# The turn between two passes: joins ahead of the values' low parts, b22's high parts earlier on ScalarE

## The chip, the core and the metric

The kernel runs on one core of a Trainium2 chip. The core has TensorE (PE, matrix products, written into eight PSUM banks of 128x512 fp32), VectorE (DVE), ScalarE (ACT), GpSimd (POOL) and SyncE (SP); each has its own queue of instructions and works through it in order. Data is moved by DMAs, issued from the queues of SP, ScalarE and GpSimd. The metric is the device time of one execution, in microseconds (us).

## The reference

```python
x = A_x                                              # 2048 tokens, 512 wide
g = sigmoid((x * gate_w).sum(-1, keepdims=True))
qkv = x @ wqkv                                       # 32 heads of 16 each
# each token attends to 8 keys: itself and those 2, 4, .. 14 tokens back
a = softmax(q . k * 16 ** -0.5) @ v, then @ wo
b = (gelu(x @ w_gate) * (x @ w_up)) @ w_down         # 1792 hidden
return g * a + (1 - g) * b
```

All inputs and outputs are fp32.

## The kernel before

**Accuracy.** TensorE is fed fp32r operands. Each fp32 operand is split into a high part (ScalarE copies it, rounded, into an fp32r tile: `hi`) and a low part (VectorE subtracts the high part from the original: `lo`), and each product takes three matmuls: high x high, low x high, high x low.

**Two passes.** The even tokens (`par` 0) go first, the odd ones (`par` 1) second. Each pass has a projection of keys and queries, then a feed-forward part, `ffn(par)`, over 14 chunks of 128 hidden columns. The projection of the values and the gate (`values`, matmuls on line 130) is spread over the first two chunks of `ffn`, the down projection over the later ones. Attention for a pass is VectorE work (scores on lines 212 and 215, the mix with the values on lines 260 to 268, a transpose on 273). It is written as one generator in small pieces, and `pull(budget)` issues the next pieces at many places among the matmuls. Most pieces are tied to a matmul (`paced`), so that they don't run before it, and have a lower priority than the code around them.

**Seven products in place of eight.** Both the keys/queries projection and the gate/up products treat their operand as a 2x2 matrix of blocks and make four block results from seven products, of sums of blocks (a scheme of Strassen's kind). The blocks of the tokens are a11, a12, a21, a22, and s1 to s4 are sums of them; those of the weights are b11, b12, b21, b22, and t1 to t4 are sums of them. The products are a11·b11, a12·b21, s1·t1, s2·t2, s3·t3, s4·b22 and a22·t4.

**The turn.** `kq_second()` makes the keys and queries of the second pass, between `ffn(0)` and `ffn(1)`. `ready()`, interleaved with the last down projections of `ffn(0)`, makes its first operands. `block(ps, a, w, ...)` issues one product: four PSUM banks, one for each 128 tokens, with six matmuls each, 24 in all. The seven blocks run in this order:

1. a11·b11 into U (banks `acc0` to `acc3`); ScalarE copies U to V_ (four `p` banks)
2. a12·b21, added to V_; V_ holds keys and queries of the first half of heads, `put` evicts it with ScalarE
3. s2·t2, added to U; ScalarE copies the sums to u2 (four `hl` tiles)
4. s3·t3, added to U; ScalarE copies the sums to u3 (four `hh` tiles)
5. a22·t4, added to U, evicted by `put` too
6. s1·t1 into Z_ (four `p` banks); VectorE adds u3 to it (`join(1, BT + t, Z_[t], u3[t])`): these are the first joins, "the sixth product's sums"
7. s4·b22, added to Z_; VectorE adds u2 (`join(1, t, Z_[t], u2[t])`): the second joins

Each `join` writes its result over the `hh` or `hl` tile, and two DMAs on GpSimd's queue store it. Block 7 adds to the same banks that the first joins read, so its first matmul on a bank comes behind the join of that bank. After block 7 TensorE goes on with the values of the second pass (line 130) and the first chunk of `ffn(1)` (line 432), whose PSUM banks are those that the second joins free.

**What sets the order.** The framework orders the instructions of each engine when the kernel is built, by their place in the program, their priority and a simulated timeline. On top of it three chains are written out by hand: `row` for VectorE, `act` for ScalarE and `mms` for TensorE (class `Row`) keep the instructions issued through them in program order on their engine. All of the turn's splits, subtractions, evictions, joins and blocks go through these chains, so all have line 760 in the profile. Attention pieces aren't in the chains, and the framework places them between.

**The values' weights.** `values_raw` loads the raw weights of a chunk kc into a `c` tile, `values_room` takes a `d` tile for its high and low parts. There are four `d` tiles; the first two chunks get theirs after t2's product, the last two after t1's.

**Buffers that matter here.** `g1` has two buffers. In the turn b11 has one and t4 the other; b22 takes b11's after block 1. s3 and s4 take the room of raw weights that are used up: s4's second pair takes that of b22.

Of the kernel before, what the change touches and what calls it, by code (L numbers as in the profile page):

```python
# [21 lines left out]
KC = D // P  # L22
# [26 lines left out]
def tile_gated_mix(ctx: ExitStack, tc: tile.TileContext, xt, wqkv, wff, wo, out):  # L49
# [11 lines left out]
    def tl(tag, dt=F32):  # L61
        return pool.tile([P, COLS.get(tag, 512)], dt, name=tag, bufs=BUFS[tag])
# [5 lines left out]
    def bank(tag):  # L68
        return psum.tile([P, 512], F32, name=tag, bufs=BUFS.get(tag, 1))
# [67 lines left out]
    def take_first(par, ps, jj, copy):  # L137

        if par not in KQ:
            KQ[par] = pool.tile([P, 3 * NP - 1, UC], F32, name="kq")  # L140
        st = tl(next(stages))[:, :CU].rearrange("p (a d) -> p a d", a=2)
        two = ps.rearrange("p (a c d) -> p c a d", a=2, c=2)
        copy(KQ[par][:, NP - 1 + jj::NP], two[:, 0])
        copy(st, two[:, 1])
        for a, t in enumerate((KS[par, 0][1, W:], QS[par, 0][1])):
            nc.sync.dma_start(t.rearrange("(p j) d -> j p d", j=NP)[jj], st[:, a])

    def shift(par, queue, i, j):
        k = KQ[par][:, :2 * NP - 1]
        if not i:  # L150
            nc.gpsimd.memset(k[:1, :NP - 1], 0.0)
        for a, b in (1, P - 15), (P - 15, P):
            queue.dma_start(k[a:b, i:j], k[a - 1:b - 1, NP + i:NP + j])

    def rows(t, jj):
        return t.rearrange("c (p j) d -> j p c d", j=NP)[jj]
# [206 lines left out]
    def fetch_d(f):  # L363
        RD[f] = tl("r")
        nc.sync.dma_start(RD[f], wff[f, :, 1024:])
# [43 lines left out]
    def fetch_sums(f):  # L409
        RAW[f] = tl("raw")  # L410
        nc.sync.dma_start(RAW[f][:, 5 * QW:7 * QW], WS[f, 1])
        q = wff[f, :, :1024].rearrange("p (a c) -> p a c", c=QW)
        nc.sync.dma_start(RAW[f].rearrange("p (a c) -> p a c", c=QW)[:, 4::3], q[:, 1::2])
# [354 lines left out]
    SRC, OP_, Q2, RAWS = {}, {}, {}, {}  # L768

    def slots(tag, n, w=512):  # L770
        t = tl(tag, F32R)
        return [t[:, i * w:i * w + 512] for i in range(n)]

    def pairs(rooms_):
        return [tuple(rooms_[2 * k:2 * k + 2]) for k in range(2)]

    def name(n, ops, srcs=None):
        for k in range(2):
            OP_[n, k], SRC[n, k] = ops[k], srcs[k] if srcs else ops[k][1].bitcast(F32)

    def halves(t):
        return t[:, :512], t[:, 512:1024]

    def hi(n, k):
        return act.activation(OP_[n, k][0], SRC[n, k], AF.Copy)

    def lo(n, k):
        h, l = OP_[n, k]
        row.tensor_tensor(l, SRC[n, k], h.bitcast(F32), op=OP.subtract)

    def both(f, *ns):
        for n in ns:
            for k in range(2):
                f(n, k)

    def sub(o, a, b):
        row.tensor_tensor(o, a, b, op=OP.subtract)
# [4 lines left out]
    def block(ps, a, w, first, kcs=(0, 1), ask=0.0):  # L802
        for t in range(BT):
            for kc in kcs:
                ah, al = OP_[a, kc]
                wh, wl = OP_[w, kc]
                for n, (a_, w_) in enumerate(((ah, wh), (al, wh), (ah, wl))):
                    mm(ps[t], t, a_, w_, first and kc == 0 and n == 0, kc == 1 and n == 2)
            if ask:
                pull(ask)  # L810

    def out_of(o, ps):
        act.activation(o, ps, AF.Copy)

    def join(par, jj, ps, s):
        row.tensor_tensor(s, ps, s, op=OP.add)
        two = s.rearrange("p (a c d) -> p a c d", a=2, c=2)
        queue = nc.gpsimd if par else nc.sync
        queue.dma_start(rows(KS[par, 1][:, W:], jj), two[:, 0])
        queue.dma_start(rows(QS[par, 1], jj), two[:, 1])  # L820
# [16 lines left out]
    def load(n, i, t, m):  # L837
        nc.sync.dma_start(tiled(t, m), TS[n][i:i + m].rearrange("i p c -> p i c"))
# [218 lines left out]
    def load_pairs(n):  # L1057
        t = [tl("d", F32R) for _ in range(2)]
        for k in range(2):
            OP_[n, k] = t[k][:, :512], t[k][:, 512:1024]  # L1060
            load(n, 2 * k, t[k], 2)
# [35 lines left out]
    def kq_second():  # L1097
        for _ in Q2["turn"]:
            pass
        q, s12 = Q2["q"], Q2["s12"]  # L1100
        t4 = slots("g1", 4)
        name("t4", pairs(t4), halves(RAWS["b21"]))
        U = [bank(f"acc{t}") for t in range(BT)]
        for k in range(2):
            X[1, 1, k] = tl("rt", F32R), tl("rt", F32R)
        name("a21", [X[1, 1, k] for k in range(2)], [q[k][2] for k in range(2)])

        block(U, "a11", "b11", True, ask=ASK[0])
        V_ = [bank("p") for _ in range(BT)]
        for t in range(BT):  # L1110
            out_of(V_[t], U[t])
        both(hi, "a22")
        both(hi, "t3")
        both(lo, "t3")
        for k in range(2):
            sub(q[k][0], q[k][0], q[k][2])
        both(hi, "s3")
        both(lo, "s3")
        name("b22", pairs(slots("g1", 4)), halves(RAWS["b22"]))
        load_pairs("t1")  # L1120
        block(V_, "a12", "b21", False, ask=ASK[1])

        def put(jj, ps):
            take_first(1, ps, jj, lambda o, i: act.activation(o, i, AF.Copy))

        def values_raw(*kcs):
            for kc in kcs:
                SRC["v", kc] = raw = tl("c")[:, :WQ + CU]
                nc.sync.dma_start(raw[:, :CU], wqkv[1, 2, :, kc * WQ:kc * WQ + CU])
                nc.sync.dma_start(raw[:, CU:CU + WQ], wqkv[0, 2, :, kc * WQ:(kc + 1) * WQ])  # L1130

        def values_room(*kcs):
            for kc in kcs:
                t = tl("d", F32R)
                WC[1, kc] = OP_["v", kc] = t[:, :WQ + CU], t[:, VL:VL + WQ + CU]
                hi("v", kc)
                lo("v", kc)

        for k in range(2):
            for part in OP_["t2", k]:  # L1140
                sub(SRC["t4", k], SRC["t4", k], part.bitcast(F32))
        both(lo, "a22")
        u2 = [tl("hl")[:, :512] for _ in range(BT)]
        u3 = [tl("hh")[:, :512] for _ in range(BT)]
        block(U, "s2", "t2", False, ask=ASK[2])
        for t in range(BT):
            out_of(u2[t], U[t])
        for t in range(2):
            put(t, V_[t])
        both(hi, "t4")  # L1150
        both(lo, "t4")
        values_raw(0, 1, 2)
        block(U, "s3", "t3", False, ask=ASK[3])
        for t in range(BT):
            out_of(u3[t], U[t])
        for t in range(2, BT):
            put(t, V_[t])
        shift(1, nc.sync, 0, BT - 1)
        both(hi, "b22")
        both(lo, "b22")  # L1160
        for k in range(2):
            sub(q[k][1], q[k][1], s12[k])
        both(hi, "s4", "a21")
        both(lo, "s4", "a21")
        values_raw(3)
        for f in range(2):
            fetch_sums(f)
        fetch_d(0)
        values_room(0, 1)
        block(U, "a22", "t4", False, ask=ASK[4])  # L1170
        for t in range(BT):
            put(BT + t, U[t])
        shift(1, nc.sync, BT - 1, NP - 1)
        done.add((1, 0))
        steps = chain(operands(1, 0, 0), operands(1, 0, 1))
        next(steps)
        Z_ = [bank("p") for _ in range(BT)]
        block(Z_, "s1", "t1", True, ask=ASK[5])
        values_room(2, 3)
        for t in range(BT):  # L1180
            join(1, BT + t, Z_[t], u3[t])
        next(steps)
        block(Z_, "s4", "b22", False, ask=ASK[6])
        for t in range(BT):
            join(1, t, Z_[t], u2[t])
        for _ in steps:
            pass
        done.add((1, 2))
# [8 lines left out]
    keep(0)  # L1197
    ffn(0)
    kq_second()
    ffn(1)  # L1200

# [42 lines left out]
```

## Time and profile before

| what | us |
|---|---|
| median of 3 runs | 605.09 (604.99 to 607.28) |
| profiled execution | 606.6 |
| its span, first to last instruction | 604.6 |
| TensorE busy | 594.1 |
| VectorE busy | 531.8 |
| ScalarE busy | 392.7 |
| GpSimd busy | 89.2 |

Rows of a timeline read: start, length, engine, line, operation, output tile <- input tiles, shape, count; in brackets the idle time before it and what ended it. PE is TensorE, DVE VectorE, ACT ScalarE, POOL GpSimd, SPq the queue of SyncE. Instructions that follow each other are merged, and one begins some 0.1 us before the one ahead of it ends, so that the cost of one in a row is read from start to start. The granted clock is a share of TensorE's full clock.

### The profile page before, as it was taken

The numbers are of one execution on the slowest core, as the hardware profiler recorded it, in microseconds if no ns is written. First come the engines' busy times: TensorE is split into PE (matmuls) and PEld (weight loads), VectorE is DVE, ScalarE is ACT, GpSimd is POOL, SyncE is SP. The second block draws the span as 40 slices with busy tenths as digits, with TensorE's granted clock in tenths as the row PEclk, the third lists the DMA queues.
The fourth block names the chain that finished last, engine by engine and source line by source line (L and its number), as shares of the span: only waits on it lengthen the run. The fifth ranks groups of instructions, "written<-read, shape, count | busy, mean of one in ns | idle before, by whom it ended". The sixth has DMA issues, their size and how long they took to land.

```text
span 604.6 us, 8205 instructions
## 1 busy us (share of the span) xinstructions
PE 594.1 (98%) x2778; PEld 494.9 (82%) x2778; DVE 531.8 (88%) x618; ACT 392.7 (65%) x670; POOL 89.2 (15%) x121
## 2 busy tenths in 40 slices
PE   8999999999999999999979999999999999999997
PEld 6889977788888887888868998888888888888886
DVE  5997979999898998899889988899999998799962
ACT  6845557787678766878672357577677666885432
POOL 0501001111111111202008001111111111101300
PEclk9999999999999999999998999999999999999999
DMA  8788886999889898888679639696877697638924
GB/s 318 256 252 243 244 271 175 270 247 255 243 240 262 220 257 227 233 290 301 224 218 288 189 116 323 141 267 174 240 184 220 170 260 173 171 110 219 167 64 155
DMA packets 80449, 134.18 MB, mean 222 GB/s; under 512 B 8092, under 2 KB 46362, under 8 KB 80152
## 3 DMA queue, kind: packets, MB, share of 16 engines
q1 hardware_dynamic: 62890, 97.67, 49.5%
q0 software_dynamic: 12576, 32.97, 27.6%
q10 hardware_dynamic: 4942, 3.01, 1.6%
q8 instruction: 22, 0.36, 0.3%
q14 instruction: 19, 0.16, 0.1%
HBM read 68.30 MB, written 38.86 MB: 177 GB/s over the span
## 4 chain that ended last, share of the span: by engine, by line
PE 83%; DMA 7%; issue 5%; ACT 2%; DVE 1%; POOL 0%; SPq 0%; POOLq 0%; ACTq 0%
PE p L432 36%; PE p L475 11%; PE acc L475 10%; PE acc L130 7%; PE acc L760 6%; PE p L693 5%; PE p L760 5%; DMA ws<-g 2%; PE acc L693 2%; DMA d<-r 2%; DMA vs<-c 1%; DMA raw<-xt 1%; DMA v<-vs 1%; DMA g<-ws 1%; POOL g L390 0%
## 5 line engine op out<-in xcount | busy, mean ns | idle before, releaser
L432 PE MATMUL p<-S,g 128*128 128x512 f32 x672 | 165.8, 390 | 0.1
L432 PEld LDWEIGHTS p<-S,g 128*128 128x128 f32 x672 | 125.4, 188 | 26.5 <-ACT rt L491 0.5
L432 PE MATMUL p<-A,g 128*128 128x512 f32 x504 | 126.9, 390 | 0.0
L432 PEld LDWEIGHTS p<-A,g 128*128 128x128 f32 x504 | 94.2, 188 | 19.9 <-DVE c L442 0.3
L212 DVE TENSOR_TENSOR prod<-kq 128x2048 f32<-128x2048 f32 x32 | 73.2, 2287 | 17.1 <-PE p L432 4.9
L390 POOL DMA_DIRECT2D g<-raw x40 | 34.5, 864 | 340.1 <-ACT g L389 208.3
L260 DVE TENSOR_TENSOR prod<-v,lg 128x2048 f32<-128x2048 f32 x32 | 72.9, 2278 | 3.2 <-DMA v<-vs 1.2
L215 DVE TENSOR_REDUCE lg<-prod 128x128 f32<-128x2048 f32 x32 | 73.1, 2283 | 0.3
L475 PE MATMUL p<-d,hh 128*128 128x512 f32 x224 | 68.1, 390 | 0.5 <-ACT hh L448 0.5
L475 PE MATMUL acc<-d,hh 128*128 128x512 f32 x224 | 61.4, 391 | 1.2 <-DMA d<-r 0.6
L475 PEld LDWEIGHTS acc<-d,hh 128*128 128x128 f32 x224 | 41.8, 188 | 11.3 <-DMA d<-r 1.4
L475 PEld LDWEIGHTS p<-d,hh 128*128 128x128 f32 x224 | 41.9, 188 | 9.7 <-ACT hh L448 0.9
L394 ACT ACTIVATE g<-raw 128x1024 fp32r<-128x1024 f32 (+1 forms) x40 | 39.5, 989 | 14.8 <-PE p L432 14.8
L389 ACT ACTIVATE g<-raw 128x1024 fp32r<-128x1024 f32 (+1 forms) x40 | 39.4, 985 | 14.5 <-PE p L760 7.8
L437 ACT ACTIVATE s<-p 128x512 f32<-128x512 f32 x56 | 33.2, 592 | 19.8 <-PE p L432 16.9
L442 DVE TENSOR_TENSOR c<-p,s 128x512 f32<-128x512 f32 x56 | 38.0, 681 | 6.8 <-PE p L432 6.6
L475 PE MATMUL p<-d,hl 128*128 128x512 f32 x112 | 42.6, 389 | 0.0
L449 DVE TENSOR_TENSOR hl<-c,hh 128x512 fp32r<-128x512 f32 x56 | 38.3, 684 | 4.7 <-ACT hh L448 4.5
L446 DVE TENSOR_TENSOR c<-c 128x512 f32<-128x512 f32 x56 | 38.3, 684 | 4.0 <-ACT c L543 3.6
L448 ACT ACTIVATE hh<-c 128x512 fp32r<-128x512 f32 x56 | 35.0, 624 | 7.8 <-DVE c L446 7.4
L264 DVE TENSOR_TENSOR prod<-prod 128x1024 f32<-128x1024 f32 x32 | 39.0, 1219 | 0.3
L130 PE MATMUL acc<-d,A 128*128 128x256 f32 (+1 forms) x288 | 37.9, 281 | 0.0
(180 smaller groups left out, 922.2 us busy)
## 6 DMA issues: line engine op xcount, KB each, us to landing
g<-raw POOLq DMA_DIRECT2D x27, 512.0 KB, 6.0
raw<-wff SPq DMA_DIRECT2D x42, 256.0 KB, 3.1
ws<-g SPq DMA_DIRECT2D x14, 768.0 KB, 5.8
g<-ws SPq DMA_DIRECT2D x14, 768.0 KB, 5.7
r<-wff SPq DMA_DIRECT2D x28, 256.0 KB, 4.1
d<-r POOLq DMA_DIRECT2D x24, 256.0 KB, 6.7
g<-raw POOLq DMA_DIRECT2D x13, 384.0 KB, 5.7
v<-vs SPq DMA_DIRECT2D x8, 512.0 KB, 7.1
```

Of the source, the lines that this page charges most:

```text
L130: LAST[:] = [nc.tensor.matmul(ps[:, :cn], a[:, t], w[:, c0:c0 + cn], start=(kc == 0 and n == 0), stop=(kc == KC - 1 and n == 2))]
L212: paced(nc.vector.tensor_tensor(prod, spans(k, jj), q[:, jj:jj + 2, None, :].to_broadcast([P, 2, W, UC]), op=OP.mult))
L215: nc.vector.tensor_reduce(two_of(lg, jj), prod.rearrange("p j w (h d) -> p (j w) h d", d=DH), axis=AX.X, op=OP.add)
L260: paced(nc.vector.tensor_tensor(prod.rearrange("p j w (h d) -> p (j w) h d", d=DH), spans(v, jj).rearrange("p j w (h d) -> p j w h d", d=D ...
L264: nc.vector.tensor_tensor(prod[:, :, :4], prod[:, :, :4], prod[:, :, 4:], op=OP.add)
L389: nc.scalar.activation(lo, raw, AF.Copy, scale=-1.0)
L394: ins = nc.scalar.activation(hi, raw, AF.Copy)
L432: LAST[:] = [nc.tensor.matmul(ps, w_, a_, start=(start and kc == 0 and n == 0), stop=(kc == 1 and n == 2), skip_group_check=True)]
L446: nc.vector.tensor_tensor(ge, ge, up, op=OP.mult)
L475: ins = nc.tensor.matmul(pp, a[:, ts], w, start=(i == 0 and n == 0 and gr == 0), stop=(i == 1 and n == 2), skip_group_check=True)
L693: ins = nc.tensor.matmul(pa, a, b, start=(first and n == 0), stop=(last and n == 2), skip_group_check=True)
L760: return lambda *args, **kw: self.add(getattr(self.eng, name)(*args, **kw))
```

## The change

Two moves within the turn:

- `name("b22", ...)` and `load_pairs("t1")` stand earlier, ahead of s3's operands, and b22's high parts (`both(hi, "b22")`, two ScalarE instructions) come with them. Before, they stood behind the evictions of block 4 and the last two `put` of V_. b22's low parts stay where they are.
- The low parts of the values' weights (`lo("v", kc)`, four VectorE instructions, one for each chunk) leave `values_room` and come behind the first four joins.

```diff
         both(hi, "a22")
         both(hi, "t3")
         both(lo, "t3")
+        name("b22", pairs(slots("g1", 4)), halves(RAWS["b22"]))
+        load_pairs("t1")
+        both(hi, "b22")
         for k in range(2):
             sub(q[k][0], q[k][0], q[k][2])
         both(hi, "s3")
         both(lo, "s3")
-        name("b22", pairs(slots("g1", 4)), halves(RAWS["b22"]))
-        load_pairs("t1")
         block(V_, "a12", "b21", False, ask=ASK[1])
...
                 WC[1, kc] = OP_["v", kc] = t[:, :WQ + CU], t[:, VL:VL + WQ + CU]
                 hi("v", kc)
-                lo("v", kc)
...
         shift(1, nc.sync, 0, BT - 1)
-        both(hi, "b22")
         both(lo, "b22")
...
         values_room(2, 3)
         for t in range(BT):
             join(1, BT + t, Z_[t], u3[t])
+        for kc in range(KC):
+            lo("v", kc)
         next(steps)
         block(Z_, "s4", "b22", False, ask=ASK[6])
```

The names: `q[k]` are the raw token blocks, `KC` is 4, `BT` is 4, `steps` makes the first gate/up operands of `ffn(1)`.

## The prediction

> **What bounds the kernel now.** I read the page's busy times and its chain, then the list of TensorE's waits, then the timelines of TensorE, VectorE and ScalarE around the longest of them.
>
> ```profile
> span 604.6 us, 8205 instructions
> PE 594.1 (98%) x2778; PEld 494.9 (82%) x2778; DVE 531.8 (88%) x618; ACT 392.7 (65%) x670; POOL 89.2 (15%) x121
> ...
> PE 83%; DMA 7%; issue 5%; ACT 2%; DVE 1%; POOL 0%; SPq 0%; POOLq 0%; ACTq 0%
> ```
>
> ```profile
> PE p L760 <- DVE hh L760: 3.4, 1, 3.4
> ```
>
> TensorE is busy for 98% of the span and makes 83% of the chain that ended last, so a microsecond is won only where TensorE stands still or runs slowly. The list of TensorE's waits is led by one that came once: a block of the turn (line 760 records all of the turn's helpers) waits 3.4 us for a VectorE result in tile hh. Its place, on TensorE's timeline:
>
> ```profile
> 302.38 5.60 PE L760 MATMUL acc<-g,A 128*128 128x512 f32 x24
> 307.82 5.60 PE L760 MATMUL p<-d,S 128*128 128x512 f32 x24
> 316.84 8.30 PE L760 MATMUL p<-g,S 128*128 128x512 f32 x24 [3.42 <-DVE hh L760]
> 324.98 0.89 PE L130 MATMUL acc<-d,A 128*128 128x258 f32 x6
> 325.70 1.56 PE L432 MATMUL p<-A,g 128*128 128x512 f32 x6
> ```
>
> The same by stretch: length, then busy times of TensorE, its weight loads, VectorE, ScalarE and GpSimd, then the granted clock, the DMA share and GB/s.
>
> ```profile
> 307.82:313.26 5.44, 5.44 (x25) 4.32 (x23) 5.44 (x7) 4.97 (x14) 0.00 (x0) 1.00 0.50 148
> 313.26:316.84 3.58, 0.16 (x1) 0.03 (x1) 3.58 (x7) 2.22 (x4) 0.07 (x1) 0.82 0.94 246
> 316.84:324.98 8.14, 8.14 (x24) 6.50 (x25) 8.11 (x11) 0.58 (x1) 7.17 (x10) 0.66 1.05 280
> 318.00:319.00 1.00, 1.00 (x4) 0.81 (x3) 0.97 (x3) 0.00 (x0) 1.00 (x3) 0.50 1.14 267
> ```
>
> The turn's last three blocks are a22·t4 (302.38), s1·t1 (307.82) and s4·b22 (316.84). A block of 24 matmuls takes 5.44 us at full clock. s4·b22 could follow at 313.26, but it starts at 316.84 (3.58 us lost) and takes 8.14 us, since the clock stood at 0.50 after the pause (the row from 318; 0.66 over the block), which loses 2.70 us more. The stall costs 3.58 + 2.70 = 6.28 us.
>
> s4·b22 adds to the banks that hold s1·t1, so it waits until the first join has read its bank. Why that join is late stands on VectorE's timeline, and on ScalarE's below it:
>
> ```profile
> 299.55 1.28 DVE L760 TENSOR_TENSOR g<-S,g 128x512 fp32r<-128x512 f32 x2
> 304.83 1.29 DVE L760 TENSOR_TENSOR g<-S,g 128x512 fp32r<-128x512 f32 x2 [3.99 <-ACT g L760]
> 306.04 1.28 DVE L760 TENSOR_TENSOR raw<-raw,r 128x512 f32<-128x512 f32 x2
> 307.24 2.29 DVE L260 TENSOR_TENSOR prod<-v,lg 128x2048 f32<-128x2048 f32 x1
> 309.44 1.29 DVE L760 TENSOR_TENSOR S<-raw,S 128x512 fp32r<-128x512 f32 x2
> 310.65 1.29 DVE L760 TENSOR_TENSOR rt<-raw,rt 128x512 fp32r<-128x512 f32 x2
> 311.85 1.22 DVE L264 TENSOR_TENSOR prod<-prod 128x1024 f32<-128x1024 f32 x1
> 312.99 1.90 DVE L760 TENSOR_TENSOR d<-c,d 128x514 fp32r<-128x514 f32 x3
> 314.80 0.69 DVE L266 TENSOR_TENSOR prod<-prod 128x512 f32<-128x512 f32 x1
> 315.40 0.69 DVE L760 TENSOR_TENSOR d<-c,d 128x514 fp32r<-128x514 f32 x1
> 316.01 2.48 DVE L760 TENSOR_TENSOR hh<-p,hh 128x512 f32<-128x512 f32 x4
> 318.40 0.42 DVE L268 TENSOR_TENSOR o<-prod 128x256 f32<-128x256 f32 x1
> ```
>
> ```profile
> 293.07 1.29 ACT L760 ACTIVATE S<-raw 128x512 fp32r<-128x512 f32 x2 [2.39 <-DVE raw L760]
> ...
> 304.13 1.19 ACT L760 ACTIVATE g<-S 128x512 fp32r<-128x512 f32 x2
> 306.82 1.23 ACT L760 ACTIVATE S<-raw 128x512 fp32r<-128x512 f32 x2 [1.50 <-DVE raw L760]
> 307.96 1.14 ACT L760 ACTIVATE rt<-raw 128x512 fp32r<-128x512 f32 x2
> ...
> 312.78 1.31 ACT L760 ACTIVATE d<-c 128x514 fp32r<-128x514 f32 x2 [0.47 <-PE p L760]
> ```
>
> VectorE ends t4's low parts (299.55) at 300.83 and stands idle for 3.99 us, because b22's low parts (304.83) wait for b22's high parts, which ScalarE makes only at 304.13, behind the evictions of s3·t3. Then come s4's subtractions (306.04), the low parts of s4 and a21 (309.44, 310.65), four low parts of the values' weights (d<-c), three attention pieces (lines 260, 264, 266), and only at 316.01 the joins. The first join could have run once its bank was full, at 307.82 + 5.44/4 = 309.18.
>
> **The change part by part.** Nothing is added or removed; six instructions of 0.6 us move, and two loads.
>
> *b22's high parts earlier on ScalarE.* The pair (1.19 us) now stands between t3's high parts and s3's, which began at 293.07 after 2.39 us of idle, so from 290.68. It ends near 291.9 and s3 isn't touched: cost 0. Without that idle time it would push s3 back by 1.19 us. Its target is b11's old buffer; the block that read it, a11·b11, is over, since ScalarE has copied that block's banks before t3's parts. At 304.13 ScalarE reaches s4's high parts directly.
>
> *The name and t1's loads* move up past ScalarE and VectorE work alone. SP issues the loads in the same place among its own; they wait for d tiles that the down products free, which doesn't change. Cost 0.
>
> *VectorE from 300.83.* b22's low parts run at once: 1.21 us (start to start, 304.83 to 306.04), to 302.04. s4's subtractions, 1.20, end at 303.24, ahead of ScalarE. ScalarE makes s4's high parts from 304.13 (1.14 us from start to start) and a21's by 306.4. VectorE fills the gap with the piece of line 260 (2.20 us), to 305.44, then s4's and a21's low parts, 1.21 + 1.20, to 307.85. That is before 309.18: VectorE then waits for TensorE, not the other way round. The joins follow TensorE at about 309.3, 310.6, 311.9 and 313.4; pieces of 264 (1.14) and 266 (0.60) fit between. Were all three remaining pieces of this stretch (264, 266, 268 at 0.42) and another 260 (2.20) run before the joins, 4.36 us in all, the first join would end at 307.85 + 4.36 + 0.62 = 312.8, still before 313.26. So s4·b22 starts at 313.26, with no pause before it to lower the clock, and ends at 318.70. Gain 3.58 + 2.70 = 6.28 us.
>
> *The values' low parts, moved behind the joins* (1.81 + 0.61 = 2.42 us), are what is late next. The value products need them, and these now start at 318.70. The last join can't begin before 313.26, so the low parts run from about 314.0 to 316.4, 2.3 us early. Their high parts are no obstacle: the second pair (312.78) ends at 314.1. If the pieces of 266, 268 and 260 (3.22 us) come in ahead, they end at 319.6 and TensorE waits up to 1 us; the same holds for the next join, of hl, which frees the bank of line 432's first product, wanted at 318.70 + 0.72. Between 0 and 1 us; I take 0, since the gaps between the joins hold two of those pieces.
>
> *GpSimd's queue.* The joins' K and Q writes are issued there, up to 6.7 us sooner, so they may stand ahead of the accumulating load that shared the queue with them:
>
> ```profile
> 316.77 0.88 POOL L390 DMA_DIRECT2D g<-raw  x1 [32.38 <-DVE hh L760]
> ```
>
> ```profile
> 340.54 1.55 PE L432 MATMUL p<-A,g 128*128 128x512 f32 x6
> ```
>
> ```profile
> g<-raw POOLq DMA_DIRECT2D x27, 512.0 KB, 6.0
> ```
>
> Issued at 316.77, it lands 6.0 us later; TensorE first reads that group at 340.54, which becomes 334.3. Eight writes of about 1 us ahead of it bring it to 330.8: cost 0.
>
> *Is the gain kept to the end?* TensorE gets 6.28 us ahead, VectorE only the 3.99 us of idle, so VectorE lags by 2.3 us more afterwards.
>
> ```profile
> 324.98:345.00 20.02, 20.02 (x142) 18.73 (x141) 18.12 (x16) 7.89 (x19) 5.91 (x9) 1.00 0.76 228
> ```
>
> ```profile
> 591.53 0.69 DVE L88 TENSOR_TENSOR hl<-raw,hh 128x512 fp32r<-128x512 f32 x1 [6.52 <-ACT hh L87]
> ```
>
> ```profile
> 595.48 0.62 PE L693 MATMUL p<-S,hh 128*128 128x512 f32 x2
> ```
>
> VectorE is idle for 1.90 us of the next 20, so most of the lag is made up by 345 us. The last attention result (591.53) is ready at 592.2, and TensorE wants it at about 596.2 (after three of the matmuls from 595.48): 4.0 us of slack at the end, more than the lag. All is kept.
>
> The sum is made against the profiled execution, which took 606.6 us: 606.6 − 6.28 = 600.3. The median of the runs is 605.09, 1.5 below, and the highest run is 607.28, so the cost of the pause may differ from run to run. From the median the sum is 598.8 if its run had the slow clock too, 601.5 (605.09 − 3.58) if not. I take 600.2, between the two and at the profile's own sum.
>
> [...]
>
> **The rivals.**
> *The median run before had no slow clock* (0.14). For it: the median is 1.5 us below the profiled run, though 2.70 us would be needed. Only the pause is won: 601.5.
> *A shorter wait takes the old one's place* (0.10), at the values' low parts or the bank of the first product: 1 us, or 2 us with the lag, so 601 to 602; with a slow clock behind it 603 to 604.
> *Hidden anyway, no change* (0.06): attention sets the end. Were VectorE's last result not to move, the slack of 4.0 us would be won and no more: 601; with a pause and slow clock there, 604.
> *Slower* (0.06): the order after the turn is planned anew, and attention's pieces slip behind. Place: the last mix; price: each microsecond beyond the slack. It decides from 4.0 + 6.3 = 10.3 us of slip, and 13.3 make the kernel 3 us slower, 608. Against it: VectorE's idle time. A slip of the values' low parts can't do it, since the attention pieces that could come before them are the few counted above.
> The forecast itself has 0.64.
>
> **How the numbers follow.** About 0.5% (3.0 us) is what a measurement here tells from no change, so faster means under 602.06. Faster: 0.64, 0.10 of the 0.14, and 0.05 of the others, 0.79. Slower: 0.06. The rest, 0.15, is within. Range: 597.6 (598.8 less 1.2, as a block wholly at 0.50 would have lost 5.44 us and not 2.70; I go not quite half that way) to 603.0, between the short wait without and with a slow clock.
>
> **What would show it.** Right: no wait of TensorE on hh in the turn; s4·b22 directly behind s1·t1 at 5.44 us; the clock at 1.00 throughout; VectorE's 3.99 us gap gone, and joins one by one 1.36 us apart, each waiting for TensorE; the value products start near 318.7. Wrong: a wait of TensorE on tile d or hl after s4·b22; ScalarE's pair at 290.67 waiting for a buffer; a wait on hl in the last 20 us; or a clock of 0.50 anywhere.

## The result, and the profile after

| | median, us | runs | ratio to before (95%) |
|---|---|---|---|
| before, measured beside it | 605.34 | 7 (604.31 to 607.28) | |
| changed | 602.48 | 7 (599.45 to 603.05) | 0.9936 (0.9913 to 0.9959) |
| changed, a second time | 601.21 | 6 (599.06 to 602.52) | 0.9934 (0.9915 to 0.9954) |

The kernel is 0.64% faster, the direction that was forecast and a time inside the range. (The ratio is estimated from all runs and is not that of the two medians: the medians differ by 2.86 us, the means by 3.86.) But the forecast was 600.2, and the profiled execution took 602.86 where the sum said 606.6 − 6.28 = 600.3. So the profile has to show two things: that the turn's 6.28 us are gone, and where 2.5 us came back.

The page of the changed kernel, its busy times and chain:

```profile
span 601.0 us, 8207 instructions
PE 591.8 (98%) x2778; PEld 493.1 (82%) x2778; DVE 531.1 (88%) x618; ACT 391.9 (65%) x670; POOL 89.3 (15%) x121
...
PE 65%; DMA 12%; issue 11%; DVE 7%; ACT 2%; SPq 1%; POOL 1%; ACTq 0%; POOLq 0%; DVEq 0%
```

TensorE's busy time fell from 594.1 to 591.8: the same 2778 matmuls, without the stretch at half clock. The rest of the 3.6 us of span, 1.3 us, is idle time that went. The share of DMA and VectorE in the chain rose.

TensorE's waits, longest sums first; the wait on hh in the turn is not among them:

```profile
PE acc L475 <- DMA d<-r: 1.8, 2, 1.2
...
PE p L475 <- DVE hl L449: 1.0, 1, 1.0
```

TensorE's timeline at the turn, in the mix of feed-forward and attention behind it, and at the end:

```profile
303.06 5.60 PE L760 MATMUL acc<-g,A 128*128 128x512 f32 x24
308.50 5.60 PE L760 MATMUL p<-d,S 128*128 128x512 f32 x24
313.94 5.60 PE L760 MATMUL p<-g,S 128*128 128x512 f32 x24
319.38 3.75 PE L130 MATMUL acc<-d,A 128*128 128x258 f32 x30
...
376.35 1.07 PE L475 MATMUL p<-d,hh 128*128 128x512 f32 x4
378.43 0.73 PE L475 MATMUL p<-d,hl 128*128 128x512 f32 x2 [1.01 <-DVE hl L449]
...
591.77 0.61 PE L693 MATMUL p<-S,hh 128*128 128x512 f32 x2
```

By stretch, with the columns of the prediction's table (the granted clock is the third number from the right):

```profile
308.50:313.94 5.44, 5.44 (x26) 4.51 (x25) 5.44 (x7) 3.81 (x10) 2.11 (x4) 1.00 0.74 211
313.94:319.38 5.44, 5.44 (x26) 4.51 (x25) 5.37 (x8) 1.00 (x2) 4.49 (x7) 1.00 1.09 301
319.38:339.40 20.02, 20.02 (x142) 18.76 (x141) 18.83 (x21) 7.81 (x19) 6.60 (x9) 1.00 0.97 286
```

s4·b22 follows s1·t1 without a pause and takes 5.44 us at full clock. Set matmul by matmul against the kernel before (both run 2778 of them, and the k-th of one is compared with the k-th of the other), the difference is this:

- *At the turn's entry*: +0.67 us (s1·t1 at 308.50, not 307.82). That lies upstream of the change, in the two waits on d<-r above, 0.6 and 1.2 us near 198 and 230, where before had one of 0.6. Such waits differ between executions; in the experiments below the entry lies anywhere from −1.47 to +1.23 us.
- *Over the turn*: −6.29 us, so −5.62 after it. The prediction's 6.28.
- *Between 376 and 384*: 1.91 us are given back, which leaves −3.71, and that is kept to the end (the row of 591.77 stood at 595.48).

So 606.6 + 0.67 − 6.29 + 1.91 = 602.9, the profiled time. The 1.91 is the thing to explain.

VectorE's timeline, in the turn and then at the place where the second unit of the second pass's attention, unit (1,1), begins (line 212 multiplies keys and queries):

```profile
300.22 2.49 DVE L760 TENSOR_TENSOR g<-S,g 128x512 fp32r<-128x512 f32 x4
...
305.50 1.29 DVE L760 TENSOR_TENSOR S<-raw,S 128x512 fp32r<-128x512 f32 x2 [1.59 <-ACT S L760]
306.71 1.28 DVE L760 TENSOR_TENSOR rt<-raw,rt 128x512 fp32r<-128x512 f32 x2
307.92 2.28 DVE L260 TENSOR_TENSOR prod<-v,lg 128x2048 f32<-128x2048 f32 x1
310.12 0.68 DVE L760 TENSOR_TENSOR hh<-p,hh 128x512 f32<-128x512 f32 x1
...
314.14 0.69 DVE L760 TENSOR_TENSOR hh<-p,hh 128x512 f32<-128x512 f32 x1
314.74 1.90 DVE L760 TENSOR_TENSOR d<-c,d 128x514 fp32r<-128x514 f32 x3
...
369.36 2.29 DVE L212 TENSOR_TENSOR prod<-kq 128x2048 f32<-128x2048 f32 x1 [3.14 <-DMA kq<-qs]
```

The 3.99 us gap became one of 1.59 us, four joins run at 310.12 to 314.14, and the values' low parts come behind them. But VectorE now waits 3.14 us for the load of unit (1,1)'s keys and queries. In the kernel before it did not wait there at all:

```profile
365.94 2.28 DVE L212 TENSOR_TENSOR prod<-kq 128x2048 f32<-128x2048 f32 x1
```

The last of these loads: KB, then us from issue to landing, first before and then changed.

```profile
kq<-qs SPq DMA_DIRECT2D x1, 512.0 KB, 5.8
```

```profile
kq<-qs SPq DMA_DIRECT2D x1, 512.0 KB, 11.1
```

And the queues around it, before (SyncE's and GpSimd's):

```profile
359.91 0.42 SPq L193 DMA_DIRECT2D kq<-qs  x1
360.44 0.36 SPq L196 DMA_DIRECT2D v<-vs  x1
361.76 0.32 SPq L385 DMA_DIRECT2D g<-ws  x1
...
362.79 0.87 POOL L390 DMA_DIRECT2D g<-raw  x1 [31.58 <-ACT g L389]
```

and changed:

```profile
353.40 0.34 SPq L196 DMA_DIRECT2D v<-vs  x1
356.13 0.32 SPq L385 DMA_DIRECT2D g<-ws  x1
358.26 0.43 SPq L193 DMA_DIRECT2D kq<-qs  x1
...
357.18 0.92 POOL L390 DMA_DIRECT2D g<-raw  x1 [28.66 <-ACT g L389]
```

The loads that follow TensorE (g, freed by its products) moved 5.6 us up with it, and the values' 7.0; the keys moved up only 1.65. Their tile is freed by VectorE's last score product of the unit before, and that stayed where it was, first before and then changed:

```profile
354.98 2.29 DVE L212 TENSOR_TENSOR prod<-kq 128x2048 f32<-128x2048 f32 x1
```

```profile
355.07 2.29 DVE L212 TENSOR_TENSOR prod<-kq 128x2048 f32<-128x2048 f32 x1
```

In the changed kernel the first of the keys' three loads goes out as this product ends, at 357.42. In the kernel before the tile was free at 357.3, and the loads stood behind stores in SyncE's queue until 358.95:

```profile
348.18 10.67 SPq L162 DMA_DIRECT2D vs<-c  x6
```

So, with VectorE's product where it was, the keys could not have moved up further. In the kernel before they go out ahead of the other three loads, in the changed one behind or beside them. With the 5.8 us of before, the load issued at 358.26 would have landed at 364.1, ahead of VectorE, which is ready for it at 366.2: it is the landing that is late, not the issue.

### The profile page after: what moved, and what is told of

The parts are those of the page before. It is cut to its first block, busy times and chain, and to the rows that moved or that the text cites. A ratio compares the mean times of both kernels' runs of the same rounds, so it can differ in the third digit from the quotient of the medians.

```text
span 601.0 us, 8207 instructions
## 1 busy us (share of the span) xinstructions
PE 591.8 (98%) x2778; PEld 493.1 (82%) x2778; DVE 531.1 (88%) x618; ACT 391.9 (65%) x670; POOL 89.3 (15%) x121
## 4 chain that ended last, share of the span: by engine, by line
PE 65%; DMA 12%; issue 11%; DVE 7%; ACT 2%; SPq 1%; POOL 1%; ACTq 0%; POOLq 0%; DVEq 0%
PE p L432 26%; PE p L475 9%; PE acc L475 8%; PE acc L760 6%; PE p L693 5%; PE p L760 5%; PE acc L130 4%; DMA d<-r 3%; DMA kq<-qs 3%; DMA ws<-g 3%; DVE prod L212 3%; PE acc L693 2%; DVE lg L215 1%; DMA g<-raw 1%; DMA vs<-hl 1%
## 5 line engine op out<-in xcount | busy, mean ns | idle before, releaser
L491 ACT ACTIVATE rt<-p 128x512 f32<-128x512 f32 x48 | 28.2, 593 | 15.3 <-PE p L475 15.2
```

## Experiments on the turn

**One part alone: b22's high parts early, the values' low parts where they were.**

```diff
+        name("b22", pairs(slots("g1", 4)), halves(RAWS["b22"]))
+        load_pairs("t1")
+        both(hi, "b22")
...
-        name("b22", pairs(slots("g1", 4)), halves(RAWS["b22"]))
-        load_pairs("t1")
...
-        both(hi, "b22")
```

> Only the first part: b22's high parts move up, the values' low parts stay ahead of the joins. My theory: b22's low parts start at 300.8 and VectorE's gap of 4 us goes, but the four values' low parts and the attention pieces between them still stand ahead of the joins, so the first join ends at about 315.3 and TensorE pauses for about 2.0 us before s4 b22 (3.58 before). Behind the turn the planned order is that of the kernel before (keys loaded ahead of values), so nothing is given back there. If a pause of 2.0 us leaves the clock at 1.00, 4.3 us are won against the kernel before; if it lowers it as the 3.58 us did, 1.5 us. Rival theory (b22's lateness was the whole cause): no pause, 6.3 us won.

Measured: 606.96 us, ratio 1.0028 (1.0012 to 1.0043), slower. TensorE and VectorE:

```profile
306.36 5.60 PE L760 MATMUL p<-d,S 128*128 128x512 f32 x24
316.86 8.56 PE L760 MATMUL p<-g,S 128*128 128x512 f32 x24 [4.90 <-DVE hh L760]
```

```profile
307.98 1.29 DVE L760 TENSOR_TENSOR d<-c,d 128x514 fp32r<-128x514 f32 x2
...
312.61 0.69 DVE L760 TENSOR_TENSOR d<-c,d 128x514 fp32r<-128x514 f32 x1 [1.02 <-DMA ks<-hh]
313.22 2.29 DVE L260 TENSOR_TENSOR prod<-v,lg 128x2048 f32<-128x2048 f32 x1
315.43 0.69 DVE L760 TENSOR_TENSOR d<-c,d 128x514 fp32r<-128x514 f32 x1
316.03 2.48 DVE L760 TENSOR_TENSOR hh<-p,hh 128x512 f32<-128x512 f32 x4
```

VectorE has its 3.99 us back, and the first join runs at 316.03 all the same. The last two low parts of the values' weights stand ahead of the joins, and their high parts start on ScalarE only at 311.97 (two in 1.14 us), since their tiles are freed near the end of s1·t1 and two copies of the next weights (lines 389 and 394) are ahead of them there. (The bracket at 312.61 names a store of keys, but the low part can't come before its high part.) The time won ahead goes to attention's pieces (264, 266 and 268 in the rows left out, then 260) and a wait. Both theories missed: the pause is 4.90 us, neither 2.0 nor none. Counted from the start of s1·t1, which came 1.47 us early in this execution, the first join is 1.5 us later than before (9.67 us for 8.19): between the last two low parts there now stands a piece of line 260 (2.2 us), where a piece of 0.6 us stood. So the turn becomes 1.73 us longer than that of the kernel before (TensorE is 1.47 us early at its entry and 0.26 late behind it), which is about what the runs lose. The early high parts are worth nothing while these two low parts stand ahead of the joins.

**The other part alone: the joins ahead of the values' low parts, b22 as before.**

```diff
                 hi("v", kc)
-                lo("v", kc)
...
             join(1, BT + t, Z_[t], u3[t])
+        for kc in range(KC):
+            lo("v", kc)
```

> Only the second part: the values' low parts move behind the joins, b22's high parts stay late. My theory: VectorE's gap of 4 us stays, yet the first join comes at about 311.9, ahead of 313.26, so TensorE doesn't pause, the clock stays at 1.00 and the 6.3 us are won at the turn: the order of the joins carries the gain, and b22's move gives only slack. Behind the turn the values are loaded ahead of the second keys, as in the changed kernel, and the queries later still, so about 2 us are given back near 378 and the whole gains about 4. Rival theory: with b22 late a pause of 1 us or more stays.

Measured: 603.04 us, ratio 0.9951 (0.9932 to 0.997). VectorE keeps its 3.99 us gap, and its first join comes at 311.86; TensorE's s4·b22 follows without a pause, at 313.27:

```profile
311.86 0.69 DVE L760 TENSOR_TENSOR hh<-p,hh 128x512 f32<-128x512 f32 x1
```

```profile
313.27 5.60 PE L760 MATMUL p<-g,S 128*128 128x512 f32 x24
```

The turn wins 6.2 us with this part alone. Further on 2.7 us are given back; VectorE waits 4.28 us for the keys, whose last load is issued only at 366.42 here. So the second part takes away the pause. That the first buys VectorE some time for afterwards (2.7 us are given back without it, 1.91 and 1.41 with it) rests on single executions; the intervals of the two kernels overlap.

**Only the two late low parts behind the joins**, first without and then with b22's early high parts.

```diff
                 hi("v", kc)
-                lo("v", kc)
+                if kc < 2:
+                    lo("v", kc)
...
+        for kc in range(2, KC):
+            lo("v", kc)
```

> The kernel before, with two of the four values' low parts moved behind the joins: a step between none and all. The first join should end at about 314.8 and TensorE pause for about 1.6 us. Shows whether a pause of that length lowers the clock: if the clock falls to 0.50 for 6.8 us as after the 3.58 us, the block s4 b22 takes some 8 us; if not, 5.44 us. My theory: it stays at 1.00, and the turn is 4.7 us shorter than before.

Measured: 606.18 us, ratio 1.001 (0.9991 to 1.003), no change. In its profiled execution (604.45) the pause is shorter and the clock stays up:

```profile
312.62:314.38 1.76, 0.16 (x1) 0.03 (x1) 1.76 (x4) 0.78 (x2) 0.00 (x0) 1.00 0.93 319
314.38:319.82 5.44, 5.44 (x24) 4.53 (x25) 5.44 (x10) 2.01 (x2) 5.05 (x8) 1.00 1.05 289
```

There the turn wins 4.4 us, and 2.95 go back with a wait of 4.32 us for the keys. Of its ten runs only four had a mean granted clock of 1.00 (median 604.7); six had 0.997 (606.4).

> b22's high parts early, and only the last two of the values' low parts behind the joins, the first two ahead as before. With b22 alone TensorE paused for 5.06 us: the joins stood behind the last low parts, whose high parts need the tiles that t1 leaves only at the end of s1 t1, so that no join could come before about 315. My theory: that tie is what counts, and the first two low parts ahead of the joins cost nothing: no pause, clock at 1.00, the turn 6.3 us shorter than before, as with all four moved. Rival theory (the number of low parts counts): a pause of about 1 us stays.

Measured: 600.67 us, ratio 0.9935 (0.9913 to 0.9956). No pause, the full 6.3 us, and 0.06 us given back in the profiled execution (600.32). VectorE's wait for the keys:

```profile
367.24 2.29 DVE L212 TENSOR_TENSOR prod<-kq 128x2048 f32<-128x2048 f32 x1 [1.61 <-DMA kq<-qs]
```

With the gap gone, the two late low parts are all that has to move. Its interval is nearly that of the full change.

## Experiments on the 1.9 us that came back

**The keys first in SyncE's queue.** The changed kernel, with the loads of unit (1,0)'s values ordered behind those of unit (1,1)'s keys and queries; every other queue and engine keeps its order.

```diff
-        load_slots(v, VS[par, hh][c])
+        load_slots(v, VS[par, hh][c], KQL[1, 1] if (par, u) == (1, 0) else None)
```

> The changed kernel, and the two loads of the values of the second pass's first unit stand behind the three loads of the second unit's keys and queries in SP's queue, as they did in the kernel before; no other engine's order changes. In the changed kernel's profile VectorE waits 3.14 us for these queries up to 369.4, and TensorE then waits for VectorE at 378.4, 1.9 us in all. My theory (the load's place in the queue gives the 1.9 us back): the keys and queries land in 5 to 6 us and not in 10, VectorE's wait falls under 1 us, TensorE's wait near 378 is gone, and the kernel is 1.5 to 1.9 us faster than the changed one, 5.5 to 6 us faster than before. Rival theory (VectorE has too much work behind the turn, whatever it waits for): the wait on the load goes, but TensorE still waits about 1.9 us in that region.

Measured: 601.05 us, ratio 0.9923 (0.9903 to 0.9943). The load lands in 9.4 us, not in the 5 to 6 of the theory, VectorE waits 1.94, and 0.72 are given back.

(KQL keeps each unit's load of queries, the last of its three; load_slots orders its two loads behind the one that it is given.)

**A smaller lag of VectorE.** Attention's gate step (line 170), at which VectorE waits 2.43 us for ScalarE, is put behind the softmax's reciprocal (kept in SOFT), once together with the keys first and once alone. Its row in the changed kernel:

```profile
352.60 0.17 DVE L170 TENSOR_SCALAR en<-en 128x8 f32<-128x8 f32 x1 [2.43 <-ACT en L167]
```

```diff
-        nc.vector.tensor_scalar_add(en, en, 1.0)
+        add = nc.vector.tensor_scalar_add(en, en, 1.0); par and ordered(add, SOFT[-1])
```

> The kernel with the keys loaded first, and the first VectorE step of the second pass's gate stands behind the softmax of its first unit. In the kernel with the keys first VectorE stands for 2.44 us in front of that step (it waits for ScalarE's exponential, which waits for TensorE's last values), so the last score product of the first unit ends at 357.0, its tile comes free, and the second unit's keys are loaded only then; VectorE later waits 1.94 us for them and TensorE gives 0.7 us back. My theory: without the 2.44 us the loads start about 2.3 us earlier, VectorE waits less than 0.5 us for them, TensorE gives nothing back between 345 and 390, and the whole is about 0.7 us faster than with the keys first. Rival theory: the loads take longer beside the weights' traffic, and TensorE still gives back 0.5 us or more.

> The changed kernel with the gate's VectorE step later, the values still loaded ahead of the second keys. If the lag of VectorE is the root (my theory), the tile of the first keys comes free 2.3 us earlier, so the load starts and lands 2 us earlier even behind the values, VectorE's wait of 3.14 us falls to about 1 us, and TensorE gives back less than 1 us (1.9 in the changed kernel). If the place in the queue is all that counts, the wait stays at 3 us and TensorE gives back 1.9 us.

Measured: 601.39, ratio 0.9938 (0.9923 to 0.9953), and 602.08, 0.9948 (0.9931 to 0.9965). VectorE no longer waits for the gate, and waits for the keys instead; with the step alone:

```profile
369.95 2.29 DVE L212 TENSOR_TENSOR prod<-kq 128x2048 f32<-128x2048 f32 x1 [5.39 <-DMA kq<-qs]
```

It gave back 3.06 us, more than the changed kernel; 1.24 of it is a wait of TensorE at 368 for GpSimd's g<-raw. With the keys first VectorE waited 3.15 us and 1.00 was given back. So VectorE's own lag isn't what costs the time: taken away, it turns into a longer wait for a load that lands after 12.7 us (9.2 with the keys first).

**The changed kernel a second time.**

> The changed kernel once more, beside the others on one chip: 3 to 4 us faster than before. A second profile of it shows which of its waits recur: the one of TensorE on VectorE near 378 should (1.9 us given back), the waits on the down weights near 198 and 229 may differ by 1 us.

Measured: 601.21 us (the table at the top). Load 10.5 us, VectorE's wait 2.60, given back 1.41. Of this 0.40 falls at 367.6 already, where TensorE needs GpSimd's g<-raw (issued at 357.17, landed after 10.3 us).

**Further loads behind the keys**: to the first of this section the load of ws for f = 3 was added (ws are split gate and up weights that the first pass stored, not softmax weights, as two expectations call them), and the keys were put first in the version with two low parts.

```diff
-            nc.sync.dma_start(w[:, :2 * n].bitcast(F32), WS[f, i])
+            ins = nc.sync.dma_start(w[:, :2 * n].bitcast(F32), WS[f, i]); f == 3 and ordered(ins, KQL[1, 1])
```

> The changed kernel with the loads of the values of unit (1,0) and of the fourth pair's softmax weights' source (ws, part f=3) both queued behind the keys and queries of unit (1,1) in SP's queue. Theory (the 1.9 us given back at 378 is VectorE's wait for these keys, which land late because the other loads go out ahead of them): the last keys' load lands in about 6 us after its issue (5.8 in the kernel before, 11.1 in the changed kernel, 9.4 with only the values behind), VectorE waits under 0.5 us for it at 366, TensorE gives back under 0.3 us at its line 475 matmul and ends some 5.5 us ahead of the kernel before, about 600.5 us. Rival (it is not the order but the traffic as a whole, or a wait of TensorE on the late ws load takes its place): keys still land in over 8 us, or TensorE waits near 368 for g, and at least 1 us of the 5.6 us is still given back, 601 to 602.5 us.

Measured: 600.32 us, ratio 0.9929 (0.9908 to 0.995). The last load lands in 7.8 us, not 6, and VectorE waits 1.55. It gives back 0.99 us, of which this is 0.69:

```profile
377.10 3.01 PE L432 MATMUL p<-A,g 128*128 128x512 f32 x12 [0.69 <-DVE c L442]
```

Neither theory had this cause: with the ws load moved, the framework orders the matmuls from 368 on in another way, and this wait comes with that order.

> The version with all of the fourth quarter's high parts moved up but only the two late low parts behind the joins, and with the loads of the values of unit (1,0) queued behind the keys and queries of unit (1,1). Theory: no pause at the turn, clock 1.00, some 6.3 us ahead there; VectorE's wait for the keys near 366 is 1.6 us or less, under the 1.25 us or so from which TensorE gives anything back, so that nearly all 6.3 us are kept: 599.8 to 600.7 us, the lowest of these kernels. Rival (the low gift-back of the two-lows version was chance of that one execution and not its order): the keys land in 9 us or more, VectorE waits over 2 us and 1 to 2 us is given back, 601 to 602.5 us.

Measured: 601.56 us, ratio 0.9936 (0.9918 to 0.9955). Against the version with two low parts only SyncE's order differs, and the load takes longer, 10.2 us after 8.4; VectorE waits 2.41 and 0.74 us are given back. The theory missed: which of the two loads goes first is not what decides. The 0.06 given back before was in part that one execution.

**The accumulating load beside the keys.** GpSimd's g<-raw, 512 KB, now goes out at 357.18, with the keys. First it adds 64 columns of 1024 only; then it writes all 512 KB without adding. Both leave out low parts of that group, so these two kernels are for their times alone.

```diff
-        nc.gpsimd.dma_start(lo.bitcast(F32), raw, accum_op=OP.add)
+        m = 64 if (par, f, i) == (1, 2, 1) else n; nc.gpsimd.dma_start(lo[:, :m].bitcast(F32), raw[:, :m], accum_op=OP.add)
```

```diff
-        nc.gpsimd.dma_start(lo.bitcast(F32), raw, accum_op=OP.add)
+        nc.gpsimd.dma_start(lo.bitcast(F32), raw, **({} if (par, f, i) == (1, 2, 1) else dict(accum_op=OP.add)))
```

> The changed kernel, but the one accumulating load on GpSimd's queue that now goes out beside the keys of unit (1,1) (g<-raw of the third quarter's second group, issued at 357.18 in the changed kernel, 362.79 in the kernel before) adds 64 of its 1024 columns only, so the low parts of the other columns are left out of the sum. Theory (the keys land late because this load's traffic, drawn 5.6 us forward, runs on the same DMA engines): the last keys' load lands 5 to 7 us after its issue (11.1 and 10.5 in two executions of the changed kernel, 5.8 before), VectorE waits under 1 us for it near 366, TensorE gives back under 0.5 us, some 600.5 us. Rival (it is the loads on SP's queue, softmax weights' ws and the values, which stay): keys still land in 8 us or more, VectorE waits 1.5 us or more, 601 to 602.5 us.

> The changed kernel, order for order the same on every engine, but that one load writes its 512 KB plainly and doesn't accumulate (the low parts of that group are replaced by the raw weights). Theory that the adding in the transfer is what slows the others: keys land in 5 to 8 us, VectorE waits under 1.5 us, and 0.5 us or less is given back. Rival (the bytes count, however they are written): keys land in 10 to 11 us as in the changed kernel, VectorE waits 2.6 to 3.2 us, and 1.4 to 1.9 us are given back, 601 to 602.5 us.

Measured: 600.85, ratio 0.9924 (0.9898 to 0.995), and 600.78, 0.9928 (0.9906 to 0.995). VectorE at the keys, with the short load:

```profile
365.77 2.29 DVE L212 TENSOR_TENSOR prod<-kq 128x2048 f32<-128x2048 f32 x1 [1.06 <-DMA kq<-qs]
```

With 32 KB in place of 512 the keys land in 7.7 us, and VectorE's wait is the shortest of all versions that are ahead. So this load's traffic is one cause of the late landing, as far as one execution shows it, but not the whole: 5.8 isn't reached. Written plainly, the same bytes hold the keys up nearly as long (9.9 us where adding had 10.5 and 11.1; VectorE waits 1.96); by how much the adding counts, one execution can't say. The short load gives back 0.99 us nonetheless, because here too the framework changed the later order, to one with the same wait on c of 0.69 us.

**Wait and loss together.** Four executions have the same order on TensorE, VectorE, ScalarE and GpSimd, instruction by instruction. They differ in SyncE's order (keys first), in how one load is written (plain write), and in when the keys land:

| | landing, us | VectorE's wait | given back | wait less 1.22 |
|---|---|---|---|---|
| keys first | 9.4 | 1.94 | 0.72 | 0.72 |
| plain write | 9.9 | 1.96 | 0.73 | 0.74 |
| changed, second time | 10.5 | 2.60 | 1.41 | 1.38 |
| changed | 11.1 | 3.14 | 1.91 | 1.92 |

Each microsecond that VectorE waits for the keys beyond 1.22 (fitted to these four) is a microsecond that TensorE has lost by 384, at the results that VectorE makes for it (hl, c). The 0.40 us that the second execution lost at 367.6 doesn't add to this: hl comes when VectorE has it, and TensorE, later by then, waits less for it. Other orders have other thresholds, but two more pairs with one order each show the same: two low parts without and with the keys first waited 1.61 and 2.41 us and gave back 0.06 and 0.74; the late gate step with and without the keys first 3.15 and 5.39, and 1.00 and 3.06. This is the cause of the 1.91 us. That the load is late because TensorE's lead draws other loads to the same time is shown, by one execution, for one of them, GpSimd's. The remaining 2 us between 5.8 and 7.7 stay open: the version with both SyncE loads behind the keys landed at 7.8 and the one with the short load at 7.7, and the two together weren't tried. None of these versions is shown to be faster than the change, as the intervals overlap; the lowest medians are 600.32 (keys ahead of values and ws) and 600.67 (two low parts).

## Why the prediction was right, and where it was wrong

*What bounds the kernel, and the price of the stall: right.* A pause of 3.58 us and 2.70 us of slow clock were named, 6.28 together; the turn became 6.29 us shorter.

*b22's high parts at no cost: right.* s3's high parts started at 293.74, 0.67 later than before, which is the upstream delay and nothing more.

*VectorE's order: right to about a microsecond.* b22's and t4's low parts run through from 300.22, the low parts of s4 and a21 end at 307.92 (forecast 307.85). Line 260's piece went behind them and not into the gap, so that 1.59 us of wait remained. The first join came at 310.12 (forecast 309.3, and 0.67 upstream), and pieces of 264, 266 and 268 fitted between the joins. s4·b22 never waited. The joins didn't wait for TensorE one by one, as the prediction had it: VectorE worked through from the first to the last of them.

*The values' low parts at 0 of 0 to 1 us: right.* Three of them ran at 314.74 to 316.55, the fourth at 318.75 behind a piece of line 260, and the value products started on time, at 319.38. What the prediction did not see is that this move alone takes the pause away, and that the other alone takes away none of it: it worked the gain out under VectorE's gap.

*"All is kept": wrong, and this is the step that failed.* The prediction followed VectorE's lag for 20 us and checked the last result of the kernel. Most of the lag of 2.3 us was to be made up in these 20 us; VectorE's idle time there fell from 1.90 to 1.19 us, so 0.7 was. But the loss came from a load. The prediction named the queue past which loads move (GpSimd's), priced only the write-backs there, and asked of the accumulating load at 316.77 only whether TensorE gets it in time; the one at 362.79 it didn't look at. It never asked what the loads that TensorE's progress releases meet when they go out 5.6 us sooner while the keys' load, released by VectorE, moves only 1.65. That cost 1.91 us in the profiled execution and 1.41 in the second. One of its signs of being wrong, a wait of TensorE on hl after s4·b22, did come, on the feed-forward's hl at 378 and not on the turn's. The rival "a shorter wait takes the old one's place" had the size, 601 to 602, but put it at the values' low parts or the first product's bank, where nothing waited.

*The median against the profile.* The prediction gave the median run either the whole slow clock (598.8) or none of it (601.5). The 52 runs of the kernel before that were made beside the experiments show a third case. By their mean granted clock:

| mean clock | runs | median, us |
|---|---|---|
| 1.00 | 5 | 603.65 |
| 0.997 | 38 | 605.08 |
| 0.994 | 9 | 606.69 |

The profiled execution (606.6, 0.994) was of the slowest kind; the usual run was faster by 1.61 us. So the gain to be had in the median was 6.28 − 1.61 = 4.67, and less the 1.41 to 1.91 given back that is 2.8 to 3.3. The two measurements gave 2.86 and 4.15 by their medians, 3.9 and 4.1 by their means. That is rather more; both profiled executions of the changed kernel were slower than its medians, so the usual run may give back less, which no profile shows. The 4.9 us that 600.2 takes off 605.09 are near the 4.67, but as a middle between two cases of which neither is the usual run: that they agree is luck. All runs of the changed kernel had 0.999 or 1.00.

## What to carry to other kernels

When a stall of the bounding engine goes, what this engine's progress releases moves up with it (here by 5.6 us), its loads too, while what another engine releases stays (here it moved 1.65). List the loads that go out in the next stretch by who frees their tile, and look for one that will now be under way together with those drawn forward; here that is where the next wait stood (the keys' 512 KB landed after 11.1 and 10.5 us beside GpSimd's 512 KB, after 7.7 beside 32 KB, and VectorE waited 3.14, 2.60 and 1.06 us). And before a profile's stall is taken off the median, see of which kind the profiled run is: a loss that differs between runs is worth only what the usual run loses.

## What the runs showed of the hardware

*The slow clock came in steps.* In the profiled execution of before the clock stood at 0.50 for 6.82 us, beginning 2.3 us after TensorE stopped; with b22's high parts alone, after a pause of 4.90 us, again for 6.82, beginning 4.3 us after TensorE stopped:

```profile
315.57:322.39 6.82, 5.55 (x13) 4.42 (x14) 6.79 (x9) 1.85 (x2) 5.62 (x8) 0.50 1.01 257
```

```profile
316.13:322.95 6.82, 6.09 (x14) 4.81 (x15) 6.53 (x10) 0.00 (x0) 5.94 (x9) 0.50 0.89 298
```

6.82 us at half clock lower the mean of a run of 604.6 us by 0.0056, to 0.994; half as long a stretch would give 0.997, and those are the two values seen beside 1.00 in the 52 runs; no run of the kernel before at 0.997 or 1.00 was profiled. In the trace of before the stretches at full clock on either side of the slow one lasted 310.61 and 283.31 us, in that of the changed kernel the only long one lasted 597.33: to within 0.04 us these are 91, 83 and 175 times half of the slow stretch of before (6.827 / 2). That the clock changes in steps of that half is an estimate from these four lengths; what sets them, no run shows. Nor do the two falls show one fixed delay after TensorE stops: 2.3 us in the one, 4.3 in the other. The version with two low parts moved and b22 as before paused for 1.76 us in its profile, at full clock, and yet six of its ten runs had 0.997. How long the pause was in those six, no profile shows.

*The keys' load took longer beside GpSimd's.* The same 512 KB on the same queue (kq<-qs) took 5.8 us in the kernel before and 7.7 to 12.7 us in the versions above that issue it at 357 to 359, beside GpSimd's load of the same group; 7.7 was beside the short one, of 32 KB. In the joins-alone version it was issued only at 366.42, 0.9 us after that load had landed (356.57 + 8.9), and took as long as before:

```profile
kq<-qs SPq DMA_DIRECT2D x1, 512.0 KB, 5.6
```

That fits the run with the short load; it doesn't say what the other loads add.
